# A new loop order for two attention blocks, with sums that stay open longer and exponentials over two banks

## The chip, the cores and the metric

The kernel runs on one core of a Trainium2 chip. The metric is device time in microseconds, the median of several runs. The engines are named as the profile names them: PE is TensorE (matmuls), PEld its weight loads, DVE is VectorE, ACT is ScalarE, POOL is GpSimd and SP issues most DMAs.

## The reference

Two attention blocks, A and B, on separate inputs of 2048 rows and 640 columns, 32 heads of 20 columns each. The outputs stand side by side.

```python
# A: each row attends to 8 rows: itself and those 2, 4, ... 14 before it
logits = einsum("bhsd,bhswd->bhsw", q, kg) * scale       # kg, vg: gathered rows
attn = softmax(where(mask, logits, -1e9)); o = einsum("bhsw,bhswd->bhsd", attn, vg)
a = o.reshape(B, S, D) @ wo
# B: full attention
scores = einsum("bhqd,bhkd->bhqk", q, k) * Dh ** -0.5
b = einsum("bhqk,bhkd->bhqd", softmax(scores), v).reshape(B, S, D) @ wo
return concatenate([a, b], axis=-1)
```

## The kernel before

Every fp32 operand of the projections is split into two parts, and three products stand for one. First come the projections of A and B (TensorE bound), then a loop of 512 steps for B's attention, beside which GpSimd computes A's attention elementwise.

A unit of B is four heads (`GH`) by 512 queries: 8 × 4 = 32 units of 16 steps. A step `i` handles 128 keys. For it there are

- four score matmuls, each 128 keys × 512 queries for one head (`s_matmul`, in the profile `ps_st<-bq,bk`), each followed by an exponential from PSUM to SBUF on ScalarE (`s_exp`, `e<-ps_st`);
- four matmuls for the row maxima of a unit that comes 52 steps later (`m_matmul`, `ps_st<-bk,bq`), each with a maximum over 512 columns on VectorE (`mx<-ps_st`; two neighbouring banks can be reduced by one instruction over 1024);
- the value product of step `i - 2` (`b_pv`, `ps_st<-e,vb`, eight PE instructions), which adds into one bank, the sum `accs[u]`.

Before, a sum is always two steps long. When it is complete, ScalarE copies the bank: the first sum of a unit to `braw`, each later one to a buffer `more`. GpSimd then adds `more` to `braw` (issued two steps later). `more` has four buffers, `spare`, picked by the sum's number in its unit, `n % 4`.

PSUM has eight banks of 512 columns. ORDER, a string of tokens, fixes the order of the loop's first 488 steps and the bank of every matmul, and with that the program order of PE, ACT and DVE. Each engine works in that order, and a matmul waits until its bank has been read. The tokens:

- `S12`: a score pair into banks 1 and 2, two exponentials of 512;
- `Y12`: one score into bank 1 and one maximum matmul into bank 2, one exponential, one maximum of 512;
- `M3`: two maximum matmuls into banks 3 and 4, one maximum of 1024; `N16`: the same into two banks apart, two maxima of 512;
- `V`: begin the next step and do a value product; a number behind it is the bank that a new sum opens;
- `H12`: one chunk of A's output projection; `j`: a piece of a transposition for it on VectorE.

GpSimd's work is planned beside it in `begin`: at step `i` pieces of A's attention are issued until their estimated time reaches `i * STEP + AHEAD`, 2.4 us a step. The last 24 steps (`b_qk`, with two sums' steps at once) and the output projection of B follow the loop.

Of the kernel before, what the change touches and what calls it, by code (L numbers as in the profile page):

```python
# [17 lines left out]
S = 2048  # L18
# [28 lines left out]
LAG = 2  # L47
# [28 lines left out]
def attention_pair(ctx, tc, xa, wqk_a, wv_a, wo_a, xb, wqk_b, wv_b, wo_b, oa, ob):  # L76
# [648 lines left out]
    accs, raws, spare = {}, {}, []  # L725
# [29 lines left out]
    def b_pv(i):  # L755
        u, kb = divmod(i, NKB)
        g, qc = divmod(u, NQC)
        n, part = divmod(kb, 2)
# [3 lines left out]
        for j in range(GH):  # L762
            pe.matmul(acc[32 * j:32 * j + 32, :], stacks[g][2][:, kb, j * VC:j * VC + 32], P[i][j % 2][:, j // 2],
                      start=(part == 0), stop=(part == 1))
        del P[i]
        if part == 0:
            return
        del accs[u]
        if n == 0:
            raws[u] = sb.tile([128, 512], F32, tag="raw", bufs=3, name="braw")  # L770
            act.copy(raws[u], acc)
        else:
            more = spare[n % 2][:, n // 2 % 2]
            act.copy(more, acc)
            after(2, pool, raws[u], raws[u], more, ALU.add)
# [5 lines left out]
    def b_two(what, ns, one):  # L781
# [36 lines left out]
    def take(kind):  # L818

        m = None  # L820
        if kind == "S":
# [176 lines left out]
    def begin(i):  # L998
# [33 lines left out]
        "Y73H54M1Y06V3Y74M1S05VY07M4S61Y23V7Y60S15N42VN06S51H43Y27H43Y05H43Y61Y27H43H43M5Y01V2Y73S04M5VY70M3Y15S62V0Y17"
        "M3S62VY71M5S24Y30V1Y27M5S43VY07H23N46S15H23Y70H23Y14H23Y56H23M0Y74V5S63M0Y72VS63Y74N01V2Y36S05Y74VM0S36Y54V7"
        "Y03M1S64VN06S53H42Y71H42Y05H42Y36Y71H42Y05H42Y36V7Y02M4S63VS06M2Y14V7M5S03Y21VM3S05Y62V1Y07M3S25VY07M5S42H31"
        "H31Y07H31Y24Y56H31Y07H31M4S26V0Y71S23M4VY71M2S46Y50V1Y74S26N35VY07S62M3H51H51Y07H51Y62M3H51Y07H51N62V0S17M3S56"
        "VM1S75Y43V6Y70S51M2VY70S15M2Y46V0S71jM2Y54VS71jY26S35N40V7jN64S21Y03VM5S42Y10V3jY47M5jS02VY70M1S64S53N07V6Y52"
        "S01M3VY70M1S53S46N07V5Y41M2S06VY70Y61S42Y35S07Y61N45V2Y01M3S75VY07S16M3S52N07V1S63M4Y02VY73S04M5Y21V7Y03M5S42V"
        "Y04M2S15Y76V0S15M2Y74VS15Y76Y23V0Y14S56N73VY71Y24H56Y03H56S71H56N42S03H56H56N74S01V2Y37M5S04VY70S13M5Y42V0Y17"
        "S63N54VY71M5S23Y40V1Y72S36N54VY07M5S23Y41V7Y02S63N54VN06S51H23Y74H23Y05H23Y16Y74H23Y05H23Y16V7Y02M4S63VY06S13"
        "M4Y27V6S01jM4S32jVjM0S75Y43V2jY01M6S35jVS01M3S57N62V0S13S45M6VM1S34Y76V5Y03S21N46VY70M2S14S65N07V1Y26S03M4VY07"  # L1040
        "M2S64S51N70V6Y52M3S71VY70M1Y53S46Y07V5Y64M1S03VY07M3S62S51Y07V6Y52S43N71VY70M4S32Y16V0Y73M4S21VY73M1S64H50H50"
        "Y73H50Y46Y12H50Y73H50S41N62V7Y06S53Y42VM5S03Y21V4Y05M6S31VS05M2Y71S64V0M2S75Y16VM2S74Y56V1Y07M2S46VY07S64M2Y51"
        "V7Y06M2S45VY06M4S13H27H27Y60H27N13S45H27Y60H27S14N53V6Y75M1S03VY70S54M1Y36V0S75jM1jS43jVjM6S51Y24V3jY07M5S14V"
        "Y70M1S46S53N07V4Y56M1S03VY07M5S31S42N70V3S41M5S72VM0S74Y56V2Y73M0S46VY73S45M0S62N37V4Y05S36M1VY07M5S31S42N70V3"
        "Y41M5S72VY70M1S46S35N07V4S36M1S05VM6S03Y21V5Y04M6S13VY04M1S73H65H65Y04H65N73S21H65Y40H65S72N13V4Y05M6S31VY05"
        "S32M6Y14V5Y03S67Y21VM3S07Y61V2Y03M4S17VY03S16M4Y72V3Y01M4S67VS02M6S15Y43V0M6S12Y35VM6S14H52Y30H52Y16Y74H52Y30"
        "H52Y16H52M3Y70V1S25M6Y43VY02M6S54Y31V0Y24M6S53VY15M3S27Y06V5jS12jM3jS70jVM1S67Y34V0jY12M5S74VY71M2S46Y50V1Y74"
        "M2S65VY07M5S42S31N70V4Y35M6S21VY05M1S37S64N50V3Y27S16M4VY70M1S64S35N07V6Y41M2S05VS70M4S13Y26V7Y01M4S63VY06S12"
# [47 lines left out]
    for kind, *ns in re.findall("[A-Zj][0-7]*", ORDER):  # L1096
        ns = [int(n) for n in ns]
        if kind == "j":
            run_jobs(turn_jobs, 1)
# [87 lines left out]
```

## Time and profile before

| | |
|---|---|
| median of 3 runs | 1745.47 us (1745.34 to 1747.84) |
| the profiled execution | 1745.1 us, span 1742.9 us |
| granted clock of TensorE | 0.998 |
| busy share of the span: PE, DVE, ACT, POOL | 99%, 77%, 77%, 73% |
| first exponential to last row maximum | 454.8 to 1626.9 us |
| exponentials | 2048 of 512 columns, mean 630 ns |
| row maxima | 952 of 512 columns (mean 682 ns), 548 of 1024 (1216 ns) |
| copies to `more`, additions from it | 224 each, mean 610 and 1287 ns |

The mean of an instruction is its own duration. Its group's busy time counts instructions that overlap once, so busy time over count is nearer to what one costs in a queue. "Idle before" is idle time of the engine just ahead of a group's instructions, with the engine that ended it.

### The profile page before, as it was taken

The page shows a single profiled execution, that of the slowest core. Times are in us where ns is not written, and L with a number is a line of the kernel's source. Part 1 is how long each engine was busy: PE and PEld are TensorE (multiplying, and loading weights), DVE is VectorE, ACT ScalarE, POOL GpSimd, SP SyncE. Part 2 cuts the span into 40 slices and gives each one's busy share as a digit, 9 for nine tenths or more (in the row PEclk, how much of TensorE's full clock was granted, in tenths as well). Part 3 has the DMA queues.
Part 4 walks back from the last instruction along what each step waited for, and adds up shares of the span by engine and source line. Part 5 has one row for each costly group of instructions (what it writes and reads, how often), then busy time and mean ns, then how long its engine had stood idle before and what let it go on. Part 6 is the DMA issues. An engine that isn't in the chain of part 4 may idle for free.

```text
span 1742.9 us, 34666 instructions
## 1 busy us (share of the span) xinstructions
PE 1726.1 (99%) x12711; PEld 1011.2 (58%) x12711; DVE 1349.3 (77%) x1818; ACT 1337.3 (77%) x2658; POOL 1271.9 (73%) x1125
## 2 busy tenths in 40 slices
PE   9999999999999999999999999999999999999999
PEld 8988888989635544444444443444444445444568
DVE  3113232888899999999999999999999999999300
ACT  4323223232599999999999999999999999999981
POOL 0000950999899999999999999999999953545242
PEclk9999999999999999999999999999999999999999
DMA  6447878657754263445435433543642532111123
GB/s 226 120 139 242 304 258 261 219 183 219 207 152 133 91 175 119 130 127 148 128 121 158 141 126 106 176 136 110 168 137 96 142 90 55 43 36 52 34 75 113
DMA packets 194435, 248.29 MB, mean 142 GB/s; under 512 B 89308, under 2 KB 114396, under 8 KB 193272
## 3 DMA queue, kind: packets, MB, share of 16 engines
q1 hardware_dynamic: 193688, 245.41, 46.6%
q8 instruction: 100, 1.64, 0.4%
q14 instruction: 71, 0.58, 0.1%
q10 hardware_dynamic: 576, 0.66, 0.1%
HBM read 181.08 MB, written 64.91 MB: 141 GB/s over the span
## 4 chain that ended last, share of the span: by engine, by line
PE 73%; POOL 17%; DMA 4%; issue 3%; DVE 2%; ACT 1%; SPq 1%; POOLq 0%; ACTq 0%; DVEq 0%
PE ps_st L71 73%; POOL akv L71 9%; POOL braw L71 4%; DVE mx L71 2%; POOL ao L71 1%; DMA stg<-xa 1%; SPq L71 1%; DMA mdr<-mtr 1%; DMA bq<-qb_d 1%; POOL ww L71 1%; POOL al L71 1%; ACT e L71 1%; DMA s_d<-braw 1%; POOL xn L71 0%; DMA s_d<-sm 0%
## 5 line engine op out<-in xcount | busy, mean ns | idle before, releaser
L71 DVE TENSOR_REDUCE mx<-ps_st 128x1 f32<-128x512 f32 (+1 forms) x1500 | 1227.5, 877 | 72.5 <-PE ps_st L71 61.4
L71 ACT ACTIVATE e<-ps_st 128x512 f32<-128x512 f32 x2048 | 1067.3, 630 | 32.5 <-PE ps_st L71 19.6
L71 PE MATMUL ps_st<-bk,bq 60*128 60x512 f32 x2048 | 555.1, 436 | 0.5 <-DVE mx L71 0.4
L71 PE MATMUL ps_st<-bq,bk 62*128 62x512 f32 x2048 | 548.7, 431 | 3.5 <-ACT e L71 1.8
L71 PE MATMUL ps_st<-e,vb 128*32 128x512 f32 x4096 | 543.1, 604 | 0.5
L71 PEld LDWEIGHTS ps_st<-bq,bk 62*128 62x128 f32 x2048 | 276.6, 184 | 401.6 <-ACT e L71 250.2
L71 POOL TENSOR_TENSOR braw<-braw,more 128x512 f32<-128x512 f32 x224 | 288.3, 1287 | 85.6 <-ACT more L71 85.1
L71 PEld LDWEIGHTS ps_st<-bk,bq 60*128 60x128 f32 x2048 | 257.9, 184 | 102.9 <-DVE mx L71 45.1
L71 POOL TENSOR_TENSOR akv<-akv,aq 128x1280 f32<-128x1280 f32 x64 | 188.4, 2944 | 166.4 <-DMA akv<-ka_d 166.3
L71 POOL TENSOR_TENSOR akv<-akv 128x640 f32<-128x640 f32 (+3 forms) x304 | 282.6, 930 | 14.7
L71 ACT COPY ro<-ps_st 128x320 f32<-128x320 f32 (+2 forms) x172 | 73.9, 465 | 185.9 <-PE ps_st L71 104.0
L71 PE MATMUL ps_st<-ww,xn 64*128 64x320 f32 (+1 forms) x1776 | 188.1, 311 | 6.5 <-POOL xn L71 2.4
L71 PEld LDWEIGHTS ps_st<-ww,xn 64*128 64x128 f32 (+1 forms) x1776 | 175.6, 187 | 22.6 <-ACT e L71 8.3
L71 PEld LDWEIGHTS ps_st<-e,vb 128*32 128x32 f32 x4096 | 82.2, 108 | 149.9 <-issue 77.1
L71 POOL TENSOR_TENSOR akv<-akv,al 128x1280 f32<-128x1280 f32 x64 | 151.6, 2368 | 0.1
L71 ACT COPY more<-ps_st 128x512 f32<-128x512 f32 x224 | 136.7, 610 | 4.0 <-POOL braw L71 2.0
L71 PE MATMUL ps_st<-xn,w 128*128 128x512 f32 x480 | 115.8, 390 | 0.0
L71 PEld LDWEIGHTS ps_st<-xn,w 128*128 128x128 f32 x480 | 90.1, 188 | 19.4
L71 POOL TENSOR_TENSOR xn<-stg,xn 128x512 fp32r<-128x512 f32 (+1 forms) x30 | 53.8, 1804 | 62.8 <-ACT xn L71 61.5
L71 PE MATMUL ps_st<-ww,aot 64*128 64x320 f32 x960 | 99.2, 308 | 0.0
L71 ACT CAST pr<-ps_st 128x512 fp32r<-128x512 f32 x40 | 23.5, 587 | 98.7 <-PE ps_st L71 93.0
L71 PEld LDWEIGHTS ps_st<-ww,aot 64*128 64x128 f32 x960 | 91.0, 186 | 4.6 <-DVE mx L71 0.5
(65 smaller groups left out, 1042.3 us busy)
## 6 DMA issues: line engine op xcount, KB each, us to landing
akv<-ka_d SPq DMA_DIRECT2D x128, 320.0 KB
akv<-va_d SPq DMA_DIRECT2D x128, 320.0 KB
kb_d<-pr SPq DMA_DIRECT2D x20, 512.0 KB
qb_d<-pr SPq DMA_DIRECT2D x20, 512.0 KB
bk<-kb_d SPq DMA_DIRECT2D x16, 640.0 KB
bq<-qb_d SPq DMA_DIRECT2D x64, 160.0 KB
stg<-xb SPq DMA_DIRECT2D x16, 512.0 KB
rb<-s_d SPq DMA_DIRECT2D x128, 64.0 KB
```

Of the source, the lines that this page charges most:

```text
L71: return self.tc.keep_in_program_order(op(*a, **k))
```

## The change

ORDER is written anew, and there are two new tokens.

- `v` is a `V` after which the bank of the sum stays open: the next step's value product adds to it. A `V` closes the sum. A sum may so run over one to 16 steps, within one unit. `sums[u]` counts the sums of a unit, as a unit no longer has eight.
- `T2` is a score pair into banks 2 and 3 with one exponential over 1024 columns. It reads both banks in one instruction.

```diff
-    def b_pv(i):
+    def b_pv(i, keep=False):
...
-        n, part = divmod(kb, 2)
+        part = int(u in accs)
         if part == 0:
             accs[u] = bank()
...
-                      start=(part == 0), stop=(part == 1))
+                      start=(part == 0), stop=not keep)
         del P[i]
-        if part == 0:
+        if keep:
             return
         del accs[u]
+        n = sums[u] = sums.get(u, -1) + 1
...
         for (kind, i, j, r), n in zip(what, ns):
-            if kind == "s":
+            if kind == "s" and not one:
                 s_exp(i, j, r, psb[:, n])
-            elif not one or r == 1:
+            elif kind == "s" and r == 1:
+                s_exp(i, j, slice(0, 2), psb[:, n - 1:n + 1])
+            elif kind == "m" and (not one or r == 1):
...
-        if kind == "S":
+        if kind in "ST":
...
-        b_two(what, ns if len(ns) == 2 else (ns[0], ns[0] + 1), kind == "M")
+        b_two(what, ns if len(ns) == 2 else (ns[0], ns[0] + 1), kind in "MT")
...
-        "Y07M1S36Y54V0Y71S26M4Y03V7Y06M4S31Y72V0Y13M4S76VY71M2S64S05N17V6Y04M2S51VY70M4S13S26N07V1Y25S04N36VY07S25M3Y61"
+        "Y07M1Y36N54V0Y71M5M2S04V7Y06T2M4Y71v0Y26M4S73VY71M2S64Y05Y17v6Y02M3S51VY70M1S53S46N07v5Y41M2S06VY70Y61T2M4Y07"
...
-                b_pv(i - LAG)
+                b_pv(i - LAG, kind == "v")
...
-            b_pv(i - LAG - 1)
+            b_pv(i - LAG - 1, True)
             b_pv(i - LAG)
```

The tokens of the two orders:

| | S | T | Y | M | N | V | v | H | j |
|---|---|---|---|---|---|---|---|---|---|
| before | 627 | – | 698 | 444 | 127 | 488 | – | 160 | 80 |
| changed | 319 | 270 | 774 | 397 | 136 | 235 | 253 | 160 | 80 |

The first place is ScalarE's queue where one unit ends, near step 371. The numbers behind the names are those of the buffers; `more_...` is one of two tiles that hold the four buffers, and `braw` is the first sum of the next unit. Before:

```order
L71 COPY more_4767<-ps_st_66 128x512
L71 ACTIVATE e_15418<-ps_st_66 128x512
L71 ACTIVATE e_15434<-ps_st_66 128x512 x2
L71 ACTIVATE e_15443<-ps_st_66 128x512 x2
L71 ACTIVATE e_15459<-ps_st_66 128x512 x2
L71 ACTIVATE e_15464<-ps_st_66 128x512
L71 COPY more_4768<-ps_st_66 128x512
```

The same place in the changed program:

```order
L71 COPY more_4766<-ps_st_66 128x512
L71 ACTIVATE e_15313<-ps_st_66 128x512 x2
L71 ACTIVATE e_15324<-ps_st_66 128x1024
L71 COPY braw_15341<-ps_st_66 128x512
L71 ACTIVATE e_15349<-ps_st_66 128x1024
L71 ACTIVATE e_15353<-ps_st_66 128x1024
L71 ACTIVATE e_15357<-ps_st_66 128x512 x2
L71 ACTIVATE e_15380<-ps_st_66 128x1024
L71 COPY more_4766<-ps_st_66 128x512
```

Before, eight exponentials stand between two copies, and the two go to different tiles. Now four exponentials of 1024 and four of 512 stand between two copies into the same tile; as the unit that ends has six sums, both are number 1 in `n % 4` and use the same buffer, three steps apart.

The second place is VectorE's queue near the loop's 45th step, where a unit's maxima begin; `mx` holds them, `128x1` is the result of a maximum over 512 columns and `128x2` that of one over 1024. Before:

```order
L71 TENSOR_REDUCE mx_6058<-ps_st 128x2
L71 TENSOR_REDUCE mx_6058<-ps_st 128x1 x2
L71 TENSOR_REDUCE mx_6058<-ps_st 128x2
L71 TENSOR_REDUCE mx_6058<-ps_st 128x1 x9
L71 TENSOR_REDUCE mx_6058<-ps_st 128x2
```

In the changed program:

```order
L71 TENSOR_REDUCE mx_6033<-ps_st 128x2
L71 TENSOR_REDUCE mx_6033<-ps_st 128x1 x6
L71 TENSOR_REDUCE mx_6033<-ps_st 128x2
L71 TENSOR_REDUCE mx_6033<-ps_st 128x1
L71 RECIPROCAL sm<-sm 128x16
L71 TENSOR_REDUCE mx_6033<-ps_st 128x1 x4
L71 TENSOR_REDUCE mx_6033<-ps_st 128x2
```

The single maxima stand in other runs between the double ones; over the whole program there are 94 more of them, and 47 fewer double ones.

More of the change, by code (lines that the diff above doesn't have):

```diff
@@ L724, in attention_pair @@
     P = {}
-    accs, raws, spare = {}, {}, []
+    accs, raws, sums, spare = {}, {}, {}, []
     def s_matmul(i, pl, r, p):
@@ L1032, in attention_pair @@
[L1032 to L1036, printed above, removed]
@@ new lines, in attention_pair @@
+        "S03N21H74H74M5Y02V3S74M0Y56v2Y73M0T4VY73M4Y60T1v3Y76S45M1VY07T4M1Y63V7Y04Y51H62Y37H62Y04H62Y51H62Y70H62M4Y31V7"
+        "Y06S52Y34N71v0T4Y62Y73vY12M4S36VY71T2M4Y60v1M2Y74T5VS07M2H65Y41H65H65N70Y23H65H65Y74Y21V0M5S74Y32v1Y07T5N42v"
+        "Y07S63M4VY07T2M4Y61v7Y02T4N63VM0T4H62H62Y73H62Y01H62Y73Y54H62M0S73v5Y46S72M0VY74M2S60Y15v7Y60T2N14VY06S51M2Y47"
+        "v6Y50M2S14VY70H15Y24Y63H15Y07H15Y24H15Y06H15M2Y74V0Y15S76Y23N04v1T6Y53Y02vT6M3S25vjM6jT3jS02jvjM3T6Y05VY72M3T5"
+        "Y01v2Y75T3N06VY70Y13T4N62v0Y17S63M4VY71T2M4Y06V7Y13T4N02Y67v3Y04T1M5VY70Y14T5M2Y07v1Y64M2S05VY07M4Y63T1Y70v6"
@@ new lines, in attention_pair @@
+        "Y51T2Y74vY50T2N14VY70Y15T2N46v0S71M4Y32VS71N63H45Y02H45T6H45Y31H45Y02H45M6S31N02v4T6Y53Y01vM6T2Y51VM2Y07T5V4M2"
+        "T0H76Y54H76H76Y01Y23H76Y54H76M0V2Y73M4Y60T1v7Y63M4S21VY06T2M4Y17v6Y02M4S31VY70M2Y14T5v0Y71S23M5VY71T2M5Y40v1"
+        "Y72M5T3VY07Y24T5N31v7S02M3S65vjS02jM3jS61jvjY02S35N64VY06Y13S25Y47S60N13v2N17T4Y36vY70S15M3VS07M5T3Y12v0Y75N62"
+        "T3VY71S65M3Y20Y17v6Y52T3M0VY75M3S20S16N57v2Y01T3M5VY70Y13T5N42Y07v1Y63T4Y02vY73T4N26VY07M4S32Y61v7Y03S24N56V"
+        "Y05Y14H32Y76H32S05N14H32T6H32N01H32N45T6v0Y13S24N76VY71T2M4Y60v1S72M4S36vY07T4M2VM6T4H03Y12H03H03N47S65H03M1"
@@ new lines, in attention_pair @@
+        "H03Y46V7Y05M1Y34T6v5Y03S21M6VY04T2M6Y15v4Y03M6T1VY05Y13T6N24v5T0M2Y67VY04T2N16Y75V0Y14M2T6Y50v1Y74T2Y56vjS07j"
+        "M2jS46jvjY07M2T4VY07M4Y63T1v7Y06M4S12VY06M1S35S47N06v3T1M4Y07VY62S01M4S73N62v0T4Y17Y63vY75M3S12VY71S26Y53Y40"
+        "Y17N23v6S70M4S12vY70M4S31VY70S32M4S16N07v3Y24T0N56VY72S01M4Y63v7Y02S14M5VY03H41Y25Y76H41Y03Y25H41T6H41Y03H41"
+        "Y25M6V3Y04Y51T6N23v0T4M1S76vY53M1S74VY73T5M1Y40v3Y75M1S46VY07M4Y61T2v7Y06S54N32VY06Y15H43Y27H43Y06H43Y51Y27H43"
+        "H43M5Y01V2T3M5S70v1Y24S35M6VY02M3T6Y51v2S07M3Y56VY70Y13T4N62v7T0S63M4jvjT0jS62jM4vjY03S61M4VY06M2T4Y17v6Y05M2"
@@ new lines, in attention_pair @@
+        "S41VY70Y15T2Y46v0Y17T5N23VN74T1M5S30V7N41T2N05T6V4Y31Y02M6T4Y13v0Y24M6S15VY14Y52T6Y03Y41v5M6T2Y01VY74T2M0Y65v4"
+        "Y73M0S26VY75Y63T0N24V5M6S32Y01V4Y53M6H20S14H20Y35H20N17S64H20Y35H20Y16Y47v3Y02S15M6VY04M1T6S53v4M6Y02S51vM6Y50"
+        "T2VM6S51H02M3H02H02S17M5H02H02M3S17M5V0M3S72M5T0V7Y42M0Y35T6v2Y34M0S76VY73T4M0Y62v3Y74T0Y56vY42T0M6VY24Y05T6"
+        "Y13v4Y05T2N76vjT0jS57jM2jvjY06S51M2VY07T5M2Y14v7Y06S53M1VY06Y53T1N47v6Y05M3S21VY70S15S24N36Y07v1Y23T5N74VN07T2"
+        "T5N41V0N72T3T5N10v7Y42S31M5VY04M2S15T6Y40v1Y25N03T6VN02T4T6N31v0Y25S43M6VY15T3M6Y02V1N35S74H06M1H06S73H06Y54"
@@ new lines, in attention_pair @@
+        "H06Y71H06M2S45Y71v0Y62M3S15VY71T5M3S20v1M5Y74S23vY07T5N24VY07M5S23Y41v7Y02M5S34VY03H41N25S76H41Y03H41Y27H41Y56"
+        "Y03H41N72v5T3M0Y67VY42T0N36V7Y52M3Y01T6v2Y05S34M6VY03T4M6Y12v3S04jM6jS51jvjY02T6M4VY02Y17T4N63v2Y70S16Y54vjY73"
+        "S01N46VY70Y35M1S46S07N35v4S06M1Y37VY05S61M2S74N05v6S73M1Y04VY75Y03T1N46S75v0Y14M2S76vY17M4S63VY71Y62T4Y30v1M6"
+        "Y02T4VN07S63T4M1Y06v7Y53M1S04VY06Y53T1N47v6Y05M3S21VY70T1M3Y56V7Y02M3S51H67H67Y02H67N51S43H67Y02H67M4S31v0T6"
+        "S23M4vY17S26M4VY71T2M4Y60v1M2Y74T5VN07S23H65Y41H65Y02H65Y73H65M0H65Y72V3Y04M5Y71T2v4S07M5Y32vY70M5S31VY70M2Y16"
@@ new lines, in attention_pair @@
+        "T4v0Y71S23M4VY71T2M4Y60v1S72jM4jS36jvjY07T4M2VY07M4Y63T1v7Y06S54M1jVY06M4S31S27Y06v3M4Y21T6VN02T4T6Y13v0Y25T3"
+        "N76VN75T1T3N60v7Y15S62M3VY06M1S53S74Y60v5Y73M1S04vY67S03M1VY07S64M1S35N07v6Y41M2S05VY70M4S13S26N70v1T4M2S76v"
+        "Y05S72M3VY07T5M3H21H21Y07H21N65S34H21Y07H21S36M4v0Y71S23M4VY71T2M4Y06v7Y13M4S02VY06Y13T4N27v6Y03M1S54VY70H54"
+        "N31S62H54Y07H54Y63H54Y21H54M6Y03V2T4M6S01v2Y35S40M6VY13T4M6Y02v3Y41M6S05VY04Y51T6N23v4Y50S12M6VY05T1jM6jS34jv0"
+        "jS15jM6Y23vY14M6S52VY15M3S27N06S51v2Y73T4M0VY73M4Y60T1Y37v6Y52T0M3VY75M0S24S36N57v2Y01M3T5VY70M5Y14T2S07v1M2T5"
@@ new lines, in attention_pair @@
+        "Y04VY72T5M3Y01v2Y75M3S06VY70M5Y14T2V7Y01M5S23Y47v1T2N06Y54VY07T2H65Y41H65Y70H65Y13H65Y04H65M2S71N04v6T2Y75Y01v"
+        "Y52M3S71VY70T1Y53N46v0Y71T2M4VY71H62Y35Y04H62Y71H62Y35H62Y70H62M3V5Y07M1Y36T4v7Y03S21M4VY06T2M4Y17v6Y02T4Y31v"
+        "Y70T4M1VY70Y53T1Y46v0Y73T5N12vjY17S34M5VY71T2M5jS04jv1jM2T5Y07jvY26T3N05VY72S06M3S51N27v0Y63T4M1VY73M4Y62T0Y37"
+        "v6Y05T1M3VY70M1S53S46N07v5Y41M2S06VY70Y61T2M4V0M6S13T4N02v1Y73S06M4VY07Y62S35Y41N07v6T2Y51Y04vY71S52M3VY70M1T3"
+        "Y56V7Y04Y13H25Y67H25S40N13H25T6H25Y41H25Y03M6V1Y25M3S07Y61v5Y07S42Y36vY40S67M1VY06T3M1Y75v6Y04M1S73VY70Y53T1"
@@ new lines, in attention_pair @@
+        "N46v0Y75S43M1VY74H36N52S01H36Y74H36Y50H36Y21H36M4Y70V2Y13S74M5Y20v1Y73M5S24VY07T2M5Y41V0Y72T5M3Y10v2Y75T3Y16vj"
+        "S07jM3jS56jvjY70M3S15VY07M5Y14T2v7Y01S65M2VY06T4M2Y17v6Y05M2S41VY70M4S13N26S07v1Y05M3S27VY02M5S74Y31Y20v7Y63T4"
+        "M1VY06M4S31Y72v0Y13M4S76VY71T2M4Y60V7Y13M4S62S07Y13v6M4S02Y73vY01M4S27VY03Y71H24Y56H24S30N71H24T5H24Y37H24M0"
+        "Y56v7Y42M0S35VY62T3Y05N17v6S52M3Y01VS75M3S02N16v7T3Y05N12vY63T0M4VM2T0H65Y74H65Y32Y01H65Y74H65Y32H65M0Y74v3S25"
+        "M6Y01VY24S07M5Y13v2Y07M5S14VY70Y13T5Y42v0Y71M2S65vjT6jS14jM2jvjY75S16M2VY71T4M2Y60v1Y75T2Y46vY07T2M5VY07Y24T5"
@@ new lines, in attention_pair @@
+        "N31V7N02T3T5Y17v0Y24N73T5VY74Y12T5N30v4Y71S32M5VY70M2S16T4N07v1Y26S03M4VY07Y62S35S41N70v6jY75T2N04vjT0jS75jM2v"
+        "jY04S71M2VY70T4M2H16H16Y07H16N54S23H16Y07H16S52M3v0Y17S65M3VY71T5M3Y20V1M5Y74T2V0Y71Y65H23H23Y40Y17H23H23Y04M5"
+        "H23Y71V0Y24Y73T5N10v4M2S71Y56vY70T2N51vT6M2Y50VY71T2M5Y04v7Y31M5S02VY04M1Y35T6v0jT3jM1jS76jvjY53S74M1VY73H65"
+        "Y42Y01H65S73N42H65T0H65Y74H65M2Y01V4Y75M2S06Y14v5Y07S63N21VY07S64M2Y15v7Y60M2S41VY06Y15T2N47v6Y50S14M2VY70H15"
+        "N24S63H15Y07H15Y62H15Y43H15M6Y02v4Y35S07Y61VM2T0Y75v6Y42M0S53VY75S42M0Y36v5Y74M0S23VY74T2M0Y65V4Y73Y02H16Y54"
@@ L1088, in attention_pair @@
+        "S05S36M1vY57S03M1VY07Y65T1M3Y70v6Y51M3S72VY70M1S53S46N07v5Y41M2S06VY70Y61T2M4Y07v6Y13M4S02VY70M2S14S56N07v1Y25"
+        "M3S06VY07Y62T3Y51Y70v6N41T2Y05vY74T2N01VY70Y52T3N16v0Y75M1S34VY73S64S52M0N37v6S05S41N23vY70M4S32VY70T2N14T5Y07"
+        "v1Y24N73T5VY07S24M5S31N70v2Y36M4S71VY07Y16T4M2Y70v1Y64M2S75VY07M4S63S21N70v6Y52M3S71VY70M1S53S46N07v5Y41M2S06V"
+        "Y70Y61T2M4V0Y71Y62T4Y03N17v6Y52T3Y01vY75T3Y21vY75T3Y01vY75T3Y21vY75T3Y01VY75T3M1")
     owed = []
@@ L1095, in attention_pair @@
     i = 0
-    for kind, *ns in re.findall("[A-Zj][0-7]*", ORDER):
+    for kind, *ns in re.findall("[A-Zjv][0-7]*", ORDER):
         ns = [int(n) for n in ns]
@@ L1102, in attention_pair @@
             out_owed()
-        elif kind != "V":
+        elif kind not in "Vv":
             b_token(kind, ns)
```

62 lines of the change are left out of this document (8 added, 54 removed).

## The prediction

> **What bounds the kernel now.** I read the page first: TensorE is busy 99% of the span, which says little where matmuls overlap. So I cut the span at the loop that ORDER drives, from the first exponential (454.8 us) to the last row maximum (1626.9 us), and asked for each engine's busy time in it and in its two halves.
>
> ```profile
> core 0: us, PE busy (x) PEld busy (x) DVE busy (x) ACT busy (x) POOL busy (x), PEclk, DMA share, GB/s
> 454.80:1626.90 1172.10, 1167.87 (x8670) 534.00 (x8669) 1137.91 (x1588) 1134.78 (x2276) 1022.22 (x903) 1.00 0.42 120
> 454.80:1400.00 945.20, 941.92 (x7028) 432.61 (x7027) 915.92 (x1284) 915.18 (x1838) 919.50 (x805) 1.00 0.48 137
> 1400.00:1626.90 226.90, 225.95 (x1646) 101.39 (x1644) 222.00 (x305) 219.60 (x439) 102.72 (x99) 1.00 0.18 50
> 1626.90:1742.90 116.00, 111.67 (x782) 84.83 (x782) 5.16 (x12) 68.27 (x141) 34.58 (x33) 1.00 0.27 83
> ```
>
> The loop takes 1172.1 us for 488 steps, 2.40 us a step. VectorE is idle for 34.2 us of it, ScalarE for 37.3: both are 97% full, with nearly the same work. GpSimd is as full until 1400 us and half idle afterwards, and the step costs no less then (by their exponentials, four to a step, the last 226.9 us hold about 95 steps, 2.39 us each). So GpSimd keeps pace; ScalarE and VectorE set it. TensorE has room. One step's worth of it, in order of time:
>
> ```profile
> start us, us, engine line op out<-in xcount [idle before <-releaser]
> 808.96 1.06 PE L71 MATMUL ps_st<-e,vb 128*32 128x512 f32 x8
> 809.95 0.50 PE L71 MATMUL ps_st<-bk,bq 60*128 60x512 f32 x2
> 810.29 0.63 PE L71 MATMUL ps_st<-bq,bk 62*128 62x512 f32 x3
> 810.53 0.40 PE L71 MATMUL ps_st<-bk,bq 60*128 60x512 f32 x1
> 810.86 1.06 PE L71 MATMUL ps_st<-e,vb 128*32 128x512 f32 x8
> ```
>
> From one value product to the next are 1.90 us, against 2.40 us a step. The other 0.5 us are output matmuls (H) and waits for a bank. The groups of the loop alone show what fills the two full engines, and what TensorE's weight loads wait for:
>
> ```profile
> L71 ACT ACTIVATE e<-ps_st 128x512 f32<-128x512 f32 x1953 | 1019.4, 630 | 32.5 <-PE ps_st L71 19.6
> L71 ACT COPY more<-ps_st 128x512 f32<-128x512 f32 x212 | 128.5, 606 | 2.5 <-POOL braw L71 2.0 <-issue 0.3
> L71 DVE TENSOR_REDUCE mx<-ps_st 128x1 f32<-128x512 f32 x952 | 615.0, 682 | 27.7 <-PE ps_st L71 18.7
> L71 DVE TENSOR_REDUCE mx<-ps_st 128x2 f32<-128x1024 f32 x444 | 539.3, 1215 | 7.1 <-PE ps_st L71 5.2
> L71 PEld LDWEIGHTS ps_st<-bq,bk 62*128 62x128 f32 x1953 | 267.4, 184 | 397.2 <-ACT e L71 250.2 <-DVE mx L71 97.9 <-issue 17.2
> ```
>
> The circle is: TensorE waits for a bank that ScalarE or VectorE still reads, and when one of these two falls behind, the other runs dry for a moment. That moment is the 34 and 37 us.
>
> **The change, part by part.** I counted the tokens of both orders. Each has 488 V or v, 160 H, 80 j and the same 1952 score halves and 1840 maximum halves.
>
> *Wide exponentials.* S falls from 627 to 319, T (new) is 270, Y rises from 698 to 774. So 540 exponentials of 512 columns become 270 of 1024. No row of before has a wide one; these stand nearest:
>
> ```profile
> L71 ACT CAST xn<-stg 128x1024 fp32r<-128x1024 f32 x30 | 30.7, 1053 | 4.5 <-DMA stg<-xa 4.2 <-DMA stg<-xb 0.3
> L71 ACT CAST xn<-stg 128x512 fp32r<-128x512 f32 x4 | 2.5, 621 | 1.5 <-DMA stg<-xa 1.2
> 1620.12 4.52 ACT L71 ACTIVATE e<-ps_st 128x512 f32<-128x512 f32 x9
> ```
>
> 512 more columns cost 1053 − 621 = 432 ns on ScalarE. Nine exponentials in an unbroken queue took 4.52 us, so each but the last costs (4.52 − 0.63)/8 = 486 ns. Two cost 972, a wide one 486 + 432 = 918: 54 ns saved. By the group's mean (1019.4/1953 = 522 ns, waits between them not filled) a wide one costs 1062 − 108 = 954 against 1044: 90 ns saved. The lower end is nothing, since no ScalarE row reads two banks; but VectorE's does, at 1215 against 2 × 615.0/952 = 2 × 646 ns, and is not charged for it. I take 60, near the unbroken queue: 270 × 0.060 = 16.2 us of ScalarE, ends 0 and 24.3.
>
> [...]
>
> *Sums that stay open.* In the loop 243 sums were closed; now 233 are (235 V less the two that only start the loop). Ten copies of 606 ns go: 6.1 us of ScalarE. On GpSimd ten additions go:
>
> ```profile
> L71 POOL TENSOR_TENSOR braw<-braw,more 128x512 f32<-128x512 f32 x224 | 288.3, 1287 | 85.6 <-ACT more L71 85.1
> ```
>
> 10 × 1287 ns = 12.9 us, off the path as long as GpSimd only keeps pace. The ten are few because 47 sums now close after a single step, against 51 that run over three or more. Those 47 have a price. An addition comes late, because GpSimd's queue is long. Two copies and their additions, the first soon after the start and one near the end of the full stretch:
>
> ```profile
> 569.89 0.59 ACT L71 COPY more<-ps_st 128x512 f32<-128x512 f32 x1
> 580.58 1.29 POOL L71 TENSOR_TENSOR braw<-braw,more 128x512 f32<-128x512 f32 x1
> 1391.81 0.62 ACT L71 COPY more<-ps_st 128x512 f32<-128x512 f32 x1
> 1398.98 1.29 POOL L71 TENSOR_TENSOR braw<-braw,more 128x512 f32<-128x512 f32 x1
> ```
>
> They are done 11.4 and 7.8 us after their copy. The four buffers of `spare` were used again after 8 steps (19.2 us), so a copy hardly ever waited (2.0 us). Now, before GpSimd's work for A ends, one is used again after 3 steps (7.2 us), one after 4 (9.6) and eight after 5 (12.0). With 11.4 us of delay the first two copies wait 4.2 and 1.8 us, 6.0 in all; with 7.8 us, 0.6. All exponentials stand behind such a copy on ScalarE, and the value products behind those. I take the 6.0.
>
> *Maxima.* M falls from 444 to 397, N rises from 127 to 136, Y by 76. So 94 more maxima of 512 at 646 ns, +60.7 us, and 47 fewer of 1024 at 1215, −57.1: +3.6 us on VectorE, with no cover, since VectorE is full.
>
> *All else.* The matmuls are the same in number. GpSimd's A attention ends four steps earlier in the new program, by its own plan. The 116 us behind the loop and the 454.8 before it are untouched.
>
> The sum: ScalarE −16.2 − 6.1 + 6.0 = −16.3, VectorE +3.6. If ScalarE alone set the pace all of −16.3 would show, if VectorE alone +3.6. They are equally full and alternate, as the two nearly equal idle times say, so I take half of each: −6.3. The profiled execution took 1745.1 us (its span and 2.2 us around it), 0.4 below the median of 1745.47; 1745.1 − 6.3 = 1738.8, rounded to 1739.
>
> **The rivals.** *ScalarE alone sets the pace.* Then VectorE's 34.2 us of idle time give way, and the loop shortens by the 16.3: 1729. For it: TensorE's loads name ScalarE more often (250.2 us against 97.9). Against: that time also counts loads that wait while a value product runs.
>
> *VectorE sets the pace, or the new waits for `spare` eat the gain.* VectorE is full and gets 3.6 us more; ScalarE's saving becomes idle time: 1745.1 + 3.6 = 1749 at worst, about 1745 if its idle time shrinks a little. For it: 97%. Against: VectorE's waits name TensorE, which waits for banks that ScalarE holds.
>
> *Banks run out: slower.* A wide exponential gives back both banks at its end. In a queue of pairs the first bank was free after 0.52 us and the second after 1.04; now both after 0.98: 0.40 us more bank time for each of 270, 108 us. The 47 fewer wide maxima give back about 0.49 us each, 23 us. The net 85 us over 8 banks are 10.6 us of loop, if the number of free banks is what limits: 1755. The place is TensorE's weight loads for scores. It decides once an emptied queue costs ScalarE or VectorE more than the saving, that is once their idle time in the loop grows by over 6 us. For it: the 397.2 us for which those loads wait. Against: an order that runs out of banks would leave both readers idle, and they are idle 3%; and the planner could choose S wherever a bank was short, which it did 319 times.
>
> [...]
>
> **How the numbers follow.** Forecast 0.37 (1735 to 1742), ScalarE alone 0.15, no change 0.24, banks 0.24. A measurement of this kernel can tell about 0.2%, 3.5 us, from no change. The first two cases lie beyond that: faster 0.52, the same 0.24, slower 0.24. The range runs from the value of the second case less 2 us for a wide exponential that saves 90 ns in part, 1727, to the last case, 1755.
>
> **What would show it.** Right: wide exponentials at about 1060 ns alone and 0.92 to 0.95 us in a queue; ScalarE's busy time in the loop near 1110 to 1120 us, VectorE's near 1141; a loop of about 1166 us, with VectorE's idle time down to 25 and ScalarE's up to about 50; copies to `more` that wait some 6 us for GpSimd. Wrong: VectorE's idle time in the loop above 34 us, which would mean banks; or a wide exponential above 1.0 us in a queue; or waits for GpSimd of over 15 us.

## The result: 1.15% slower, and the profile after

The changed kernel took 1766.13 us (median; 1763.68 to 1769.95), the kernel before 1746.26 in the same series: a ratio of 1.0115, 95% interval 1.0094 to 1.0136. The forecast was 1739 with a range up to 1755, so the sign was wrong and the range too short. The profiled execution of the changed kernel took 1763.7 us, 18.6 more than that of before.

The page's head and its table of engines:

```profile
span 1761.9 us, 34647 instructions
PE 1732.0 (98%) x12711; PEld 994.5 (56%) x12711; DVE 1352.1 (77%) x1865; ACT 1322.8 (75%) x2378; POOL 1260.5 (72%) x1115
```

The busy times by stretch: first the loop of the changed kernel, then five pieces of 10 us out of it. The columns are those of the same view in the prediction.

```profile
core 0: us, PE busy (x) PEld busy (x) DVE busy (x) ACT busy (x) POOL busy (x), PEclk, DMA share, GB/s
454.10:1644.50 1190.40, 1172.29 (x8668) 517.65 (x8667) 1140.67 (x1635) 1119.98 (x1995) 1010.86 (x893) 0.99 0.41 118
510.00:520.00 10.00, 8.07 (x48) 2.74 (x48) 5.25 (x8) 7.05 (x12) 9.77 (x8) 0.83 0.58 171
1290.00:1300.00 10.00, 8.63 (x59) 3.58 (x55) 7.49 (x10) 9.84 (x20) 9.76 (x9) 1.00 0.48 156
1300.00:1310.00 10.00, 5.65 (x29) 2.10 (x29) 4.87 (x7) 2.27 (x6) 9.84 (x11) 0.66 0.25 84
1360.00:1370.00 10.00, 5.95 (x36) 2.09 (x34) 4.92 (x10) 4.75 (x8) 9.76 (x10) 0.80 0.09 13
1370.00:1380.00 10.00, 9.94 (x63) 3.57 (x64) 8.28 (x11) 8.15 (x16) 10.00 (x7) 0.86 0.49 151
```

The loop went from 1172.1 to 1190.4 us: 18.3 of the 18.6. ScalarE's busy time fell by 14.8 us and VectorE's rose by 2.8, much as forecast; the time still rose. It didn't rise everywhere. In three places TensorE, ScalarE and VectorE all stop while GpSimd is at its 98%, and the granted clock is 0.66 to 0.86 there, where every other piece of 10 us between 460 and 1640 us has 1.00. Around the three places, from the timeline (in brackets the idle time of the engine ahead of the line, and what ended it):

```profile
511.29 0.58 ACT L71 COPY more<-ps_st 128x512 f32<-128x512 f32 x1 [3.15 <-POOL braw L71]
511.93 0.49 PE L71 MATMUL ps_st<-bk,bq 60*128 60x512 f32 x1 [3.02 <-ACT more L71]
512.35 1.67 PE L71 MATMUL ps_st<-e,vb 128*32 128x512 f32 x8
1303.11 0.59 DVE L71 TENSOR_REDUCE am<-al 128x32 f32<-128x256 f32 x1 [5.62 <-POOL al L71]
1304.35 0.79 PE L71 MATMUL ps_st<-bk,bq 60*128 60x512 f32 x1 [5.72 <-DVE mx L71]
1305.07 1.93 PE L71 MATMUL ps_st<-e,vb 128*32 128x512 f32 x8
1308.17 3.24 ACT L71 ACTIVATE e<-ps_st 128x512 f32<-128x512 f32 x6 [7.64 <-PE ps_st L71]
1308.30 1.06 PE L71 MATMUL ps_st<-e,vb 128*32 128x512 f32 x8
1365.23 1.25 POOL L71 TENSOR_TENSOR braw<-braw,more 128x512 f32<-128x512 f32 x1
1366.52 0.58 ACT L71 COPY more<-ps_st 128x512 f32<-128x512 f32 x1 [4.25 <-POOL braw L71]
1367.15 0.79 PE L71 MATMUL ps_st<-bk,bq 60*128 60x512 f32 x1 [4.05 <-ACT more L71]
1367.88 1.93 PE L71 MATMUL ps_st<-e,vb 128*32 128x512 f32 x8
1371.32 1.79 PE L71 MATMUL ps_st<-e,vb 128*32 128x512 f32 x8
1374.82 1.06 PE L71 MATMUL ps_st<-e,vb 128*32 128x512 f32 x8
```

At 511 and 1366 us ScalarE stands before a copy to `more` whose buffer GpSimd has not yet added; the second is the reuse after three steps that the change section showed. At 1303 us VectorE stands before the head maximum of A's last tile (`am<-al`), whose input GpSimd finishes only then; every score maximum is queued behind it, so no bank comes free and TensorE stops too. In the loop of before, the copies wait 2.0 us once and the head maxima not at all.

After a stop, the value product takes 1.67 or 1.93 us where it takes 1.06 otherwise. So a stop has two prices, and both can be summed. In the timeline of matmuls TensorE's idle times at the three places are 3.02, 5.72 and 4.05 us, 12.8 together. The steps after them take 3.17, 3.23, 3.44 and 3.50 us, where steps with as many matmuls take 1.90, 1.90, 1.90 and 2.82 elsewhere, and one more takes 2.57 for 2.31: 5.1 us together. 12.8 + 5.1 = 17.9 of the loop's 18.3. The three steps in which the stops fall are another 1.7 us longer than their idle time explains, so all the rest of the change is worth little: between nothing and a gain of some 1.3 us.

In pieces of 2 us the granted clock is 0.50 from 514 to 516 us, from 1302 to 1308 and from 1366 to 1372, and 1.00 again from 518, 1308 and 1374 us on. The slower products (1.67 and 1.93 us against 1.06) agree with it, for some 4 to 6 us after each stop, also after the shortest of the three, 3.02 us. In e13 below the granted clock was 0.50 between 1316 and 1318 us, after a stop of 2.21 us. What sets the clock was not shown.

### The profile page after: what moved, and what is told of

It reads as the page before. It is cut to its first block, busy times and chain, and to the rows that moved or that the text cites. A ratio compares the mean times of both kernels' runs of the same rounds, so it can differ in the third digit from the quotient of the medians.

```text
span 1761.9 us, 34647 instructions
## 1 busy us (share of the span) xinstructions
PE 1732.0 (98%) x12711; PEld 994.5 (56%) x12711; DVE 1352.1 (77%) x1865; ACT 1322.8 (75%) x2378; POOL 1260.5 (72%) x1115
## 4 chain that ended last, share of the span: by engine, by line
PE 71%; POOL 17%; DMA 4%; DVE 3%; issue 3%; ACT 2%; SPq 1%; POOLq 0%; ACTq 0%; DVEq 0%
PE ps_st L71 71%; POOL akv L71 9%; POOL braw L71 4%; DVE mx L71 3%; ACT e L71 1%; DMA akv<-ka_d 1%; DMA bq<-qb_d 1%; POOL ao L71 1%; SPq L71 1%; DMA stg<-xa 1%; POOL al L71 1%; POOL xn L71 0%; POOL aot L71 0%; DMA s_d<-sm 0%; DMA akv<-va_d 0%
## 5 line engine op out<-in xcount | busy, mean ns | idle before, releaser
L71 ACT ACTIVATE e<-ps_st 128x512 f32<-128x512 f32 (+1 forms) x1778 | 1046.7, 679 | 49.4 <-PE ps_st L71 40.1
L71 PE MATMUL ps_st<-bk,bq 60*128 60x512 f32 x2048 | 571.1, 436 | 15.1 <-ACT more L71 8.7
L71 PE MATMUL ps_st<-bq,bk 62*128 62x512 f32 x2048 | 555.9, 434 | 2.0 <-ACT e L71 1.6
L71 PEld LDWEIGHTS ps_st<-bq,bk 62*128 62x128 f32 x2048 | 265.6, 185 | 428.0 <-ACT e L71 241.3
L71 POOL TENSOR_TENSOR braw<-braw,more 128x512 f32<-128x512 f32 x214 | 275.3, 1286 | 102.6 <-ACT more L71 102.0
L71 PEld LDWEIGHTS ps_st<-bk,bq 60*128 60x128 f32 x2048 | 265.3, 185 | 99.2 <-DVE mx L71 36.1
L71 ACT COPY more<-ps_st 128x512 f32<-128x512 f32 x214 | 127.8, 597 | 18.3 <-POOL braw L71 10.7
L71 DVE TENSOR_TENSOR pr<-ps_st,pr 128x512 fp32r<-128x512 f32 x40 | 27.6, 690 | 84.4 <-ACT pr L71 84.4
```

Source lines behind the costliest of these rows:

```text
L71: return self.tc.keep_in_program_order(op(*a, **k))
```

## The experiments

Two theories stood at first. *Waits*: the three stops are the loss, and they can be taken away. *Banks*: wide exponentials hold their banks longer, and the stops only show it. When the stops were gone, a third question was left: why does some 15 us less work on ScalarE hardly show, and would less on VectorE? Ratios below are to the kernel before, run beside each, with 95% intervals.

**The stops, one at a time.** e1_more8 gives `more` eight buffers instead of four in the first 28 units, where GpSimd has its queue:

```diff
-            more = spare[n % 2][:, n // 2 % 2]
+            k = n % (8 if u < 28 else 4)
+            more = spare[2 * (k // 4) + k % 2][:, k // 2 % 2]
...
```

> The changed kernel with eight buffers for the copies `more` in place of four (the first 28 units; the added four lie in memory that is free then). Theory (GpSimd's lateness: the changed order makes ScalarE and VectorE wait for GpSimd in three places, and each wait stops TensorE): the two waits of the copies, at 511 us (3.2 us) and 1366 us (4.3 us), go, the one of VectorE at 1303 us stays. The steps around them took 5.9 and 11.7 us more than before, of which some is regained: about 1752, 11 to 17 less than the changed kernel. Rival (banks: wide exponentials and long sums hold banks too long everywhere): no change, 1764 to 1768.

e2_due gives out the head maximum of a tile when it is due, and no earlier. The rule in `a_attention` runs the queue's first job at the tile's last piece, whatever it is. In before, that was another tile's job, and tile 15's maximum came some 3.5 steps later; in the new order the queue was empty there, and the maximum was issued in the step in which GpSimd is told to make its input. The first part of the edit keeps a tile's later step from emptying the whole queue.

```diff
+        mine = soft_jobs[-1:]
...
-        run_jobs(soft_jobs, 9)
+        while mine and mine[0] in soft_jobs:
+            run_jobs(soft_jobs, 1)
...
-                run_jobs(soft_jobs, 1)
+                if soft_jobs and soft_jobs[0][0] <= now[0]:
+                    run_jobs(soft_jobs, 1)
```

> The changed kernel, with the maximum of A's last tile issued on VectorE when it is due, not in the step in which GpSimd is told to make its input. Theory (GpSimd's lateness): VectorE's 5.6 us wait at 1303 us goes and with it the 10.8 us by which steps 338 to 354 were longer, less 3 us that are regained anyway: about 1758. Rival (banks): 1764 to 1768, the idle time only moves.

e3_both has both edits, and e4_t_as_s is the changed kernel with each `T2` written as `S23`: the same two scores with two exponentials of 512.

> Both edits in the changed kernel. Theory (GpSimd's lateness): the loss goes whole, 1742 to 1750, no gap of ScalarE or VectorE over 2 us in the loop between 500 and 1640 us. What is left against the kernel before is then what wide exponentials and other sums are worth by themselves. Rival (banks): 1760 or more.

> The changed kernel with every wide exponential taken apart: each T is an S on the same two banks, all else in place. Theory (GpSimd's lateness): the three waits stay; ScalarE has about 15 us more work, the loop gets 0 to 10 us longer: 1766 to 1776. Rival (banks held by wide exponentials): banks come free earlier, at least 10 us less, 1756 or under.

Measured: e1 1756.95 us (1.0053, 1.0041 to 1.0066), e2 1759.24 (1.0070, 1.0057 to 1.0082), e3 1747.38 (1.0006, 0.9997 to 1.0015), e4 1766.13 (1.0113, 1.0098 to 1.0129). The copies to `more` and the head maxima between 460 and 1640 us, in e1 and then in e2, say which stop each of them still has:

```profile
L71 ACT COPY more<-ps_st 128x512 f32<-128x512 f32 x202 | 120.0, 594 | 6.9 <-PE ps_st L71 4.7 <-issue 0.5 <-POOL ao L71 0.3
L71 DVE TENSOR_REDUCE am<-al 128x32 f32<-128x256 f32 x12 | 7.4, 618 | 7.7 <-POOL al L71 7.7
```

```profile
L71 ACT COPY more<-ps_st 128x512 f32<-128x512 f32 x202 | 119.8, 593 | 18.3 <-POOL braw L71 13.4 <-PE ps_st L71 2.2 <-POOL al L71 0.7
L71 DVE TENSOR_REDUCE am<-al 128x32 f32<-128x256 f32 x12 | 7.4, 618 | 0.0
```

Each edit takes its own kind of stop away and is worth 9.2 and 6.9 us; together 18.8. Alone, each leaves the other stop longer (7.7 us for 5.6 in e1), so the two gains add up to less than that. e1 gained less than the 11 to 17 us expected, and e3, inside its range, still has a gap of 3.67 us, where none over 2 us was expected. Wide exponentials (e4) are not part of the loss. That settles *waits* against *banks* for the 20 us.

**The same in the kernel before.** e7_before_both puts both edits into before, as a control; e8_before_early makes the opposite of e2 there: tile 15's head maximum is issued at once instead of as a job.

```diff
-        job(soft_jobs, 5, lambda: dve.tensor_reduce(m[:, 0], L.rearrange("p o h -> p h o"), AX.X, ALU.max))
+        if t == NT - 1:
+            dve.tensor_reduce(m[:, 0], L.rearrange("p o h -> p h o"), AX.X, ALU.max)
+        else:
+            job(soft_jobs, 5, lambda: dve.tensor_reduce(m[:, 0], L.rearrange("p o h -> p h o"), AX.X, ALU.max))
```

> The kernel before with the same two edits (eight buffers, the maximum when due). Theory (GpSimd's lateness hurts the changed order alone): its copies waited 2.0 us in all and its last maximum not at all, so no change, 1744 to 1748. If the edits speed up any order: 1740 or less.

> The kernel before, with nothing changed but that the maximum of A's last tile is put on VectorE in the step in which GpSimd is told to make its input, 3.5 steps earlier than before; it was 1.7 us clear of its input, so it will wait 6 to 7 us. Theory (such a wait stops VectorE, then TensorE and ScalarE): 1752 to 1757, 7 to 10 more than before, with a lower granted clock for some us after it. Rival (a wait of 6 us is taken up by the idle times around it): 1745 to 1749.

e7 1746.32 us (1.0004, 0.9995 to 1.0012), e8 1755.14 (1.0054, 1.0041 to 1.0068). In e8's timeline of VectorE:

```profile
1309.48 0.59 DVE L71 TENSOR_REDUCE am<-al 128x32 f32<-128x256 f32 x1 [7.35 <-POOL al L71]
```

One instruction issued too early costs 9.2 us in a kernel that has nothing else of the change; TensorE stands still for 6.98 us of them. The edits by themselves give before nothing, so e3's gain is the stops'.

**What is left of wide exponentials.** e6_both_s is e3 with each `T2` as `S23`. e9_turn_late is e3 with a last stop taken away: in e3 VectorE waits 3.67 us at 527 us for GpSimd before the transposes (`j`) of step 29, and five `j` stand two or three steps later in ORDER. e10_clean_s is e9 with `S23` for `T2`.

```diff
-Y52T3N70vjT1jS75jM3jvjY02S71M3VY70T1M3H56 ... M1T3v7Y06S51M3
+Y52T3N70vT1S75M3vY02S71M3VY70jT1jM3H56 ... M1T3v7jY06jS51jM3
```

> The changed kernel with eight buffers and the due maximum, as the run with both edits (1747.4), and every wide exponential taken apart into two. Now no wait for GpSimd covers what they are worth. If half of ScalarE's relief shows in the loop, as the prediction took it (270 x 60 ns, half of 16 us): 1754 to 1757. If ScalarE alone sets the pace: 1763. If VectorE alone sets it, or wide exponentials give back what they save by holding banks: 1746 to 1749.

> The run with both edits, and the second gap of VectorE at the start is taken away too: the five transpositions (j) of step 29, which waited 3.7 us for GpSimd at 527 us, come two to three steps later. Theory (GpSimd's lateness): the 5 us by which steps 18 to 34 are still longer shrink to 1 or 2, 1742 to 1745, the first version under the kernel before. Rival (the gap only moves): 1746 to 1749.

> The version without the gaps (both edits, later transpositions; 1744.9), with every wide exponential taken apart into two: what wide exponentials are worth in a loop without waits for GpSimd. The prediction's half: 8 more, 1753. VectorE sets the pace: 1 to 3 more, 1746 to 1748, and ScalarE's idle time in the loop falls from 50 to under 40 us while VectorE's stays at 33 to 36. Banks: 1744 or less.

e6 1749.56 us (1.0024, 1.0014 to 1.0033), e9 1744.94 (0.9992, 0.9983 to 1.0002), e10 1747.93 (1.0014, 1.0005 to 1.0023). So 270 wide exponentials are worth 2.2 us (e6 less e3) and 3.0 us (e10 less e9). Each pair is from two series; by the ratios to the kernel before it is 3.1 and 3.8 us. e10's profile also has a gap of 2.9 us that e9's hasn't. In the loop of e9, and then of e10, ScalarE's busy times differ by 13.6 us:

```profile
455.40:1625.80 1170.40, 1165.67 (x8670) 515.87 (x8667) 1139.98 (x1636) 1120.19 (x1995) 1010.71 (x893) 1.00 0.42 120
```

```profile
454.90:1632.80 1177.90, 1172.14 (x8670) 528.25 (x8669) 1141.60 (x1635) 1133.79 (x2265) 1011.02 (x892) 1.00 0.42 119
```

Single profiled loops scatter by some us (e10's executions took 1745.90 to 1749.96), so the medians decide: the order without its stops is as fast as before, and a sixth to a quarter of what ScalarE was relieved of shows. The half that the prediction took would have made e6 1754 to 1757 and e10 1753.

**Is it VectorE?** e11_clean_496 is e9, and e12_before_496 before, with every maximum of the loop over 496 of its 512 columns (16 columns of each are left out).

```diff
-psb[:, n - 1:n + 1]    psb[:, n]
+psb[:, n - 1:n + 1, :496]    psb[:, n, :496]
```

> The version without the gaps, with the loop's row maxima taken over 496 of each 512 columns (the last 16 of each bank are left out of the maximum; the products are still computed): 16 x 1.04 ns less for each of 1840, 30.7 us of VectorE. VectorE sets the pace, and ScalarE has 50 us of idle time to give: 20 to 28 less, 1717 to 1725. ScalarE or banks set it: under 8 less, 1737 or more. Half: 15 less, 1730.

> The kernel before with the same shorter maxima (496 of 512 columns; the rest as it was). In its order ScalarE has some 37 us of idle time against VectorE's 37, and no wide exponentials. VectorE sets the pace here as well: 15 to 25 less, 1721 to 1731. If ScalarE becomes the bound at once: 5 to 12 less, 1734 to 1741. The difference to the run before says what ScalarE's relief by wide exponentials is worth once VectorE has room.

e11 1743.12 us (0.9987, 0.9978 to 0.9996), e12 1744.83 (0.9993, 0.9984 to 1.0002). The groups of single maxima in the loop, of e9 and then of e11:

```profile
L71 DVE TENSOR_REDUCE mx<-ps_st 128x1 f32<-128x512 f32 x1046 | 667.5, 681 | 23.8 <-PE ps_st L71 15.8 <-ACT e L71 0.5
```

```profile
L71 DVE TENSOR_REDUCE mx<-ps_st 128x1 f32<-128x496 f32 x1046 | 654.9, 666 | 41.3 <-PE ps_st L71 24.8 <-ACT e L71 0.6
```

By these durations 16 columns are 15 ns, and over 1840 maximum halves 28 us. In the loop of e11 VectorE's busy time is 21.6 us below e9's:

```profile
456.50:1625.50 1169.00, 1161.34 (x8668) 520.39 (x8667) 1118.38 (x1635) 1118.62 (x1995) 1011.44 (x893) 1.00 0.42 120
```

1.8 us came back (0.9 by the ratios of the two series, 1.4 in the profiled loop); the rest turned into idle time before the maxima, and about half of what was added before the single ones was ended by TensorE. In before the same relief brought 0.5 us, less than either case of its expectation. Less work on VectorE alone doesn't shorten the loop.

**TensorE, GpSimd, or both.** e13_half_pv is e9 with the value products over 256 of 512 queries (the other half is left out, in the 24 steps behind the loop too), e14_less_pool is e9 with GpSimd's first product of A's attention over 128 of 1280 columns (the planner is told the old cost, so that the order stays). e15_half_less has both, and e16_half_less_s is e15 with `S23` for `T2`.

```diff
-            pe.matmul(acc[32 * j:32 * j + 32, :], ..., P[i][j % 2][:, j // 2],
+            pe.matmul(acc[32 * j:32 * j + 32, :256], ..., P[i][j % 2][:, j // 2, :256],
```

```diff
-        pool(kv, kv, q.unsqueeze(1).to_broadcast([128, 2, D]), ALU.mult)
+        gp.us += 1152 * 0.00212
+        pool(kv[:, :, :64], kv[:, :, :64], q[:, :64].unsqueeze(1).to_broadcast([128, 2, 64]), ALU.mult)
```

> The version without the gaps, with every value product over 256 of the 512 queries (the other half of each sum is left out; all else in place): about 0.45 us less of TensorE a step. Theory (TensorE sets the pace: a step's time is fixed by its number of matmuls, 1.88 us for six, 2.27 for eight, 2.76 for ten): the steps after GpSimd's work for A shorten from 2.35 to about 2.2 us, those before only to GpSimd's 2.35: 1715 to 1735. Rival (VectorE or ScalarE, which the last three runs speak against): 1740 or more.

> The version without the gaps, with GpSimd's first multiplication for A's scores over 128 of 1280 columns (the rest is left out, its planned time is kept, so the order stays): 2.5 us less of GpSimd for each of some 50 in the loop, 120 us. Theory (TensorE sets the pace): 1738 to 1746. Rival (GpSimd sets the pace until 1400 us): 1725 or less.

> Both of these reliefs at once. Theory (TensorE, and GpSimd just behind it): the loop falls to what ScalarE and VectorE need in a queue, 2.2 to 2.3 us a step: 1655 to 1700. Rival (banks or VectorE and ScalarE already set it): 1715 or more.

> The same two reliefs, with every wide exponential taken apart into two. If wide exponentials are worth their 16 us of ScalarE only once TensorE has room: 6 to 16 more than the run before. If they are worth as little as in the full loop: 0 to 3 more.

e13 1727.07 us (0.9895, 0.9880 to 0.9909), e14 1740.33 (0.9968, 0.9956 to 0.9980), e15 1702.30 (0.9749, 0.9733 to 0.9766), e16 1706.86 (0.9778, 0.9763 to 0.9792). Against e9 that is −17.9 for TensorE, −4.6 for GpSimd, and −42.6 for both. e15 just missed its range (1655 to 1700), and the 4.6 us between e15 and e16 lie between the two cases of e16. Not all of these gains lie in the loop. The loops of e13, e14 and e15:

```profile
454.50:1617.80 1163.30, 1102.82 (x8668) 542.73 (x8667) 1129.11 (x1635) 1106.61 (x1995) 1009.60 (x893) 0.99 0.43 121
452.80:1622.20 1169.40, 1164.75 (x8668) 515.59 (x8667) 1139.48 (x1635) 1119.81 (x1994) 893.90 (x887) 1.00 0.42 120
453.20:1594.50 1141.30, 1092.36 (x8668) 536.70 (x8667) 1127.80 (x1635) 1105.13 (x1995) 890.85 (x886) 1.00 0.43 123
```

The loop is 7.1, 1.0 and 29.1 us shorter than e9's, in one profiled execution each; the rest lies before and behind it (behind it, e13 and e15 save 9.4 and 10.8 us). For both reliefs together that is still far more than the sum. In e13 GpSimd is late again, among others here: ScalarE waits 3.42 us for it at 898 us, VectorE 3.70 at 1185 and ScalarE 2.59 at 1314, with TensorE at a granted clock of 0.81 to 0.85 around the three.

How far behind TensorE the others are, the 80 steps from the 401st value product on show, where GpSimd is half idle. In e9, e11 and e13:

```profile
1425.50:1612.10 186.60, 186.36 (x1327) 77.60 (x1326) 183.55 (x251) 180.67 (x328) 87.44 (x86) 1.00 0.17 47
1425.60:1612.00 186.40, 186.05 (x1328) 79.54 (x1328) 180.27 (x251) 180.54 (x328) 87.50 (x86) 1.00 0.17 47
1421.90:1604.70 182.80, 175.18 (x1325) 83.20 (x1323) 181.67 (x251) 178.22 (x328) 87.41 (x86) 1.00 0.17 48
```

Shorter maxima bring 0.2 us there, half products 3.8, though the products alone are some 0.4 us a step shorter, over 30 us in 80 steps (between 460 and 1580 us, 3736 of their instructions fill 498 us in e9, and 3760 fill 302 in e13). Then VectorE is idle for only 1.1 us of 182.8. So TensorE sets the pace, but by about 2% only; then VectorE takes over.

In the whole loop of e15 VectorE is idle for 13.5 us, against 30.4 in e9, and TensorE waits. The waits of TensorE's matmuls between 480 and 1590 us, in before and then in e15:

```profile
PE ps_st L71 <- ACT e L71: 1.8, 1, 1.8
PE ps_st L71 <- DVE mx L71: 1.0, 3, 0.4
```

```profile
PE ps_st L71 <- DVE mx L71: 16.4, 59, 0.8
PE ps_st L71 <- ACT e L71: 14.5, 57, 0.5
```

This is the circle that the prediction took the kernel before for, and it appears only once TensorE is relieved. In before, TensorE waited 2.8 us in 1110. Even in e15 wide exponentials bring only 4.6 us (e16 less e15).

## Why the prediction was wrong

**"TensorE has room" was the step that failed.** It rested on one step of 1.90 us against a mean of 2.40. That step has six score and maximum matmuls (x2, x3, x1 in its rows); a mean step has (1952 + 1840)/488 = 7.8. A step a little further on in the same timeline of before, with eight:

```profile
812.80 1.07 PE L71 MATMUL ps_st<-e,vb 128*32 128x512 f32 x8
813.80 0.50 PE L71 MATMUL ps_st<-bq,bk 62*128 62x512 f32 x1
813.80 0.50 PE L71 MATMUL ps_st<-bk,bq 60*128 60x512 f32 x1
814.14 0.39 PE L71 MATMUL ps_st<-bq,bk 62*128 62x512 f32 x2
814.37 0.43 PE L71 MATMUL ps_st<-bk,bq 60*128 60x512 f32 x2
814.64 0.40 PE L71 MATMUL ps_st<-bq,bk 62*128 62x512 f32 x1
814.64 0.45 PE L71 MATMUL ps_st<-bk,bq 60*128 60x512 f32 x1
815.12 1.07 PE L71 MATMUL ps_st<-e,vb 128*32 128x512 f32 x8
```

From product to product are 2.32 us. Over all steps of before that hold no H, the median is 1.90 us with six (293 steps), 2.31 with eight (81) and 2.82 with ten (68), and the least are 1.88, 2.27 and 2.76: the time of a step goes by its number of matmuls. The changed order has the same matmuls, and the same medians. This alone doesn't tell TensorE from its readers, as each of these matmuls is also read by an exponential or a maximum: in e15, with half products, the least times fall to 1.52, 1.96 and 2.51, but the medians stay at 1.85, 2.32 and 2.72. What tells them apart is that TensorE is idle for only 4.2 us of the loop of before, and that relief of TensorE shortens the loop (e13, e15) where relief of VectorE (e11) and ScalarE (e9 against e10) hardly does. The "other 0.5 us" were matmuls (of H and of the larger steps), hardly waits for a bank. The weight loads' 397.2 us misled: a load that waits while a product runs stops nothing here, as those 4.2 us of TensorE say. TensorE's own waits, 2.8 us, were left out. The chain of waits after 1400 us in before, where GpSimd is half idle, says the same:

```profile
by line: PE ps_st L71 86.6%; DVE mx L71 11.8%; ACT e L71 0.9%; issue 0.4%; ACT more L71 0.3%; DVE sm L71 0.1%; DVEq L71 0.0%
```

**"Both are 97% full" was read as "set the pace".** A duration holds the time that the next instruction overlaps (630 ns for an exponential, 486 in an unbroken queue), so an engine with a queue of one looks fuller than it is: 21.6 us less of VectorE's busy time only left it more idle (e11). As a measure of nearness a busy share holds here: once TensorE and GpSimd were relieved, the loop fell by 2.5% and VectorE was 99% busy. As a sign of who sets the pace it failed: VectorE's relief brought 1 to 2 us (e11), and TensorE, at 99%, had the least room.

**Half of each: −6.3.** This term rested on VectorE and ScalarE alone setting the pace. Without the stops the order measures −1.0 us of 1745.94, not to be told from none (e9).

**Wide exponentials at 60 ns.** Sound, a little high. The group in the changed kernel:

```profile
L71 ACT ACTIVATE e<-ps_st 128x1024 f32<-128x1024 f32 x270 | 279.6, 1039 | 5.1 <-PE ps_st L71 3.9 <-ACT e L71 0.3
```

1039 ns alone were forecast as 1060. In an unbroken queue a wide one starts 904 ns before what follows it (median of the trace; 920 to 950 forecast) and one of 512 columns 477 or 478 before another of its kind, 488 before a wide one: 50 to 60 ns saved a pair. The two loops of e9 and e10 give 13.6 us over 270 pairs, 50 ns.

**The waits for `more`: 6.0 us at most.** The mechanism was right, and one of the two places: 4.2 us were worked out for the reuse after three steps, 4.25 were measured, and 10.7 in all. That agreement is partly luck: the addition there ended 10.5 us after the copy, not 11.4, and the buffer was wanted again after 6.2 us, not 7.2; the row of before from that end of the loop, 7.8 us, would have given 0.6. The stop at 511 us is a reuse after six steps, which the sum took to be free: its addition ended 16.2 us after the copy. What failed above all is the price. It was added to ScalarE's own time and then halved with it. But ScalarE's wait stops TensorE, which has no room to regain it: 4.05 us idle, 2.2 us more at the lower clock, and e1 shows 9.2 us for the two.

**GpSimd "keeps pace" and its additions are "off the path".** This put VectorE's wait for GpSimd at nothing: the instructions of A on VectorE were left out of the sum. No row of the loop of before showed such a wait (VectorE's idle time before its `am<-al` is 0.0 us there), but e8's expectation worked out from the same trace that this maximum was only 1.7 us clear of its input. It waited 5.62 us, and e2 shows 6.9 us for it. The sign "waits for GpSimd of over 15 us" did come: 10.7 and 5.6 in the loop.

**The rivals.** *ScalarE alone* is refuted (e10 less e9: 3 to 4 us of some 16). *VectorE, or waits for `spare`, eat the gain* named one of the two causes, priced at 1749; the kernel took 1766. *Banks* had the right sign for a wrong reason: VectorE's idle time rose to 49.7 us, over the 34 given as the sign of banks, but without the stops it is 30.4, and e4 is no faster without wide exponentials. A sign that two mechanisms share tells neither.

**Still open.** Why two thirds or more of ScalarE's relief don't show even in e15, where TensorE waits for ScalarE 57 times; VectorE, idle for 13.5 us there and for 1.2 us of the 80 steps, is the likely cause, but no run relieved VectorE and TensorE at once. The best of the runs that compute all, e9, is not measurably faster than before.

## What to carry to other kernels

Divide the time from one landmark to the next by the work in it, over many steps, before you say that an engine has room: one step is no mean, and the busy shares of 97% and 99% here said neither full nor free. Where several engines are nearly full, shorten the work of one at a time, and of two together, and compare the loops rather than the whole times: here that told an engine that sets the pace by 2% from those behind it. When an order is made anew, list each instruction that waits for the slowest queue and ask how far behind that queue is there; a single one, some 3.5 steps early, cost 9 us here. The stops here, on a path without slack, were not to be halved: they cost their length and a third to a half more at the lower clock after them (12.8 and 5.1 us at the three places; 9.2 us for one of 6.98 in e8).

## What the runs showed of the hardware

In the changed kernel TensorE stopped for 3.02, 5.72 and 4.05 us, and its granted clock was 0.50 for 2 to 6 us then (0.66 to 0.86 over 10 us): eight value matmuls took 1.67 to 1.93 us instead of 1.06, and the steps after the three stops lost 5.1 us beside the 12.8 of standing still. One exponential over two banks of PSUM took 904 ns in a queue against 2 × 477 or more for two over one bank each, 50 to 60 ns saved.
